# Softplus as one function, and a 512-to-2048 stage in two passes over its weights, in a fused attention and two-MLP kernel

## The chip, the cores and the metric

One core of a Trainium2 chip. The metric is the device time of one execution in microseconds; the time of before is 829.03 us, the median of three runs (827.82 to 829.51).

## What is computed

Attention with a local window and 32 global tokens on 4 batches of 544 tokens, then two MLPs on the 2,176 tokens. Cut to what matters here:

```python
h = np.maximum(np.maximum(x @ w1, x @ w2), x @ w3)     # 512 -> 768
x = h @ w_out                                          # 768 -> 512
h = x @ w_in                                           # 512 -> 2048
g = np.maximum(h, 0.0) + np.log1p(np.exp(-np.abs(h)))  # softplus
out = g @ w_out2                                       # 2048 -> 512
```

The kernel computes 2,176 tokens (the first 2,176 rows of the reference's batch-by-token order). Its weights reach it as 64-bit floats and are made into pairs of 32-bit words on the chip.

## The kernel before

Every matrix operand is kept as two fp32r parts, high and low: `split` makes the high part with a copy (ScalarE, in short ACT, or VectorE, in short DVE) and the low part with a subtraction on GpSimd (in short POOL). A product is three TensorE (PE) matmuls: high by high, high by low, low by high.

The order of all instructions is written by hand (`tc.manual_schedule()`); each engine runs its queue in that order, and all DMAs are issued from SyncE's queue (SP). Work on the side is a Python generator, from which the main loops take a step now and then: `wide(x)` adds x to a debt and takes a step for each whole one, and the constants `WU`, `WD`, `VL`, `VE` are such rates.

The stages, in time: attention (`att_stream`) beside the conversion of the first MLP's weights (`dec_stream`) and its first blocks; the first MLP by blocks u of 256 or 288 tokens, `up` (768 wide, three weights, 12 matmuls for each of 18 products, accumulated in a bank of pool `pm`; `rest` takes the maximum, L527) and `down`; beside them `words` converts the second MLP's weights, whose words go to DRAM (`qd`). When attention is over, blocks 6 and 7 run together, and on the side:

- `dec_w4` makes the 512-to-2048 weights. They come as eight pairs p; of each it reads a tile of four quarters, makes sums on DVE (L676, L677, L683, L691) and splits seven operands, as Strassen's scheme with seven products in place of eight wants them. All eight are done before the next stage, in 28 buffers of pools `cp` (8) and `wp` (24).
- `load_o(t)` makes the token operands of block t (544 tokens, four blocks): four DMAs, four sums on DVE, seven splits.

Then the 512-to-2048 stage, called the z stage here: 32 iterations i over (t, j) = divmod(i, 8), token block outside, weight pair inside. An iteration is 42 matmuls of 272 columns: `prods_a(i)` (three products into three PSUM banks za, zb, zc; copy e on ACT, first add L960), `prods_c(i - 1)` (two products; adds L968, L969), `prods_b(i)` (two products; adds L981, L982 in `mid_b`). The softplus of 4 x 272 columns is Abs (`abs_a` on za, `abs_h` on the three sums h), then Exp and Ln over 1,088 columns (L992, L993), then on DVE a max with zero and an add (`fin`, L999 and L1000), which also reads za from PSUM two iterations later. The result `a` is written to DRAM (`gd`). During block t, `load_o(t + 1)` runs beside it over eight iterations.

During the last eight iterations `make_v` makes the operands of the last matrix (2048 to 512), also eight pairs of seven operands: `vread` loads, `vsum` makes four sums (DVE for the first two pairs, POOL for the other six), `vsplit` splits; here `hi_on` puts the high parts on DVE until the z stage ends.

The last stage walks `items` (token block tb of 256 tokens, pair p), blocks 0 and 1 interleaved first, then 2 to 8. For each, `sums` makes token operands (L1098 to L1100 on DVE, copies L1105 on ACT, subtractions L1106 on DVE) about three items ahead of `mults`, 21 matmuls of 256 columns; after a block's eighth item `evac` adds up its seven products and writes the output. Two blocks take all eight PSUM banks, so the third waits for the first one's evacuation.

Of the kernel before, what the change touches and what calls it, by code (L numbers as in the profile page):

```python
# [21 lines left out]
def body(ctx, tc, kq, vw, vb, qg, w1, w2, w3, w_out, w2_in, w2_out, out):  # L22
# [483 lines left out]
    def up(u, f, i):  # L506
        n = 256 + 32 * (u % 2)
        xh, xl = xs[u]
        need((i, f))
        w = W[i, f].rearrange("p t (k f) -> p t k f", k=4)  # L510
        p = pm.tile([128, 512], F32, tag="m", name="pu")[:, 0:n]
        for k in range(4):
            nc.tensor.matmul(p, lhsT=w[:, 0, k], rhs=xh[:, k, 0:n], start=(k == 0), stop=False)  # L513
            nc.tensor.matmul(p, lhsT=w[:, 0, k], rhs=xl[:, k, 0:n], start=False, stop=False)  # L514
            nc.tensor.matmul(p, lhsT=w[:, 1, k], rhs=xh[:, k, 0:n], start=False, stop=(k == 3))  # L515
        pend.append((u, f, i, n, p))
        while len(pend) > lag[0]:
            rest()
# [77 lines left out]
    wd, w4_done = [False], [False]  # L596
# [62 lines left out]
    def dec_w4():  # L659
        half = None  # L660
        qs = {}

        def read(p):
            qs[p] = dp.tile([128, 4, 256], F32, tag="raw", name="qi", bufs=3)
            nc.sync.dma_start(out=qs[p].rearrange("p a n -> p (a n)"), in_=qd["i"][p].rearrange("p a n -> p (a n)"))

        read(0)
# [35 lines left out]
        w4_done[0] = True  # L703

    def load_o(t, pool, temp):
        x = ob[t] = pool.tile([128, 7, 2, 2, 272], F32R, tag="o", name="o7", bufs=1)
        b12, b11, b22 = [temp() for _ in range(3)]
# [3 lines left out]
        yield  # L711
        split(x[:, 0], b11)
        yield
        nc.vector.tensor_tensor(b11, b12, b11, op=ALU.subtract)
        nc.vector.tensor_tensor(b12, b22, b12, op=ALU.subtract)
        split(x[:, 2], b22)
        yield
        split(x[:, 3], b11)
        yield
        nc.vector.tensor_tensor(b11, b22, b11, op=ALU.subtract)  # L720
        nc.sync.dma_start(out=b22, in_=od[t][:, 2:4, 0:272])
        split(x[:, 5], b12)
        yield
        split(x[:, 4], b11)
        yield
        split(x[:, 1], b22)
        yield
        nc.vector.tensor_tensor(b22, b22, b11, op=ALU.subtract)
        split(x[:, 6], b22)
        yield  # L730

    def early_temp():
        return dp.tile([128, 2, 272], F32, tag="tmp", name="ot", bufs=3)

    def late_temp():
        return wp.tile([128, 2, 272], F32, tag="w", name="ot")

    with tc.manual_schedule():
# [3 lines left out]
        cp = sp = None  # L742
# [11 lines left out]
        VD = 2.2  # L754
# [3 lines left out]
        VL = 2.8  # L758
        PV = 2
        VE = 1.6  # L760
# [94 lines left out]
        for u in range(6):  # L855
# [10 lines left out]
            for c in range(4):  # L866
# [7 lines left out]
                wide(VD)  # L874
# [16 lines left out]
        d4, lo0 = dec_w4(), load_o(0, op0, early_temp)  # L891
# [21 lines left out]
        for f, _ in enumerate(down_all(7)):  # L913
            if f < 6:
                free4[0] += 1
            wide(WD)
        for _ in lo0:
            pass
        need4(7)
# [5 lines left out]
        de = dctx.enter_context(tc.tile_pool(name="de", bufs=3, side="left"))  # L925
        op1 = dctx.enter_context(tc.tile_pool(name="op1", bufs=1, side="left"))

# [16 lines left out]
        gw = []  # L944

# [4 lines left out]
        def prods_a(i):  # L950
            t, j = divmod(i, 8)
# [19 lines left out]
        def prods_b(i):  # L971
# [4 lines left out]
            c["a"] = da.tile([128, 4, 272], F32, tag="a", name="a", bufs=4)  # L976
# [7 lines left out]
        def abs_a(i):  # L984
            nc.scalar.activation(pr[i]["a"][:, 0], pr[i]["z"][0], AF.Abs)

        def abs_h(i):
            nc.scalar.activation(pr[i]["a"][:, 1:4], pr[i]["h"], AF.Abs)
# [6 lines left out]
        def fin(i):  # L995
            c = pr.pop(i)
            t, j = divmod(i, 8)
# [7 lines left out]
        items = [(0, 0), (0, 1), (0, 2), (1, 0), (0, 3), (1, 1), (0, 4), (1, 2), (0, 5), (1, 3), (0, 6), (1, 4), (0, 7), (1, 5), (1, 6), (1, 7)]  # L1005
        items += [(tb, p) for tb in range(2, 9) for p in range(8)]
# [12 lines left out]
        def vsum(p):  # L1019
            e = nc.vector if p < PV else nc.gpsimd  # L1020
            q = vq[p]
            s = vs[p] = wp.tile([128, 4, 256], F32, tag="w", name="vs")
            e.tensor_tensor(s[:, 0:2], q[:, 0:4:2], q[:, 1:4:2], op=ALU.add)
            e.tensor_tensor(s[:, 2], q[:, 0], q[:, 3], op=ALU.add)
            e.tensor_tensor(s[:, 3], q[:, 1], q[:, 3], op=ALU.subtract)
            e.tensor_tensor(q[:, 2], q[:, 2], q[:, 0], op=ALU.subtract)

        def vsplit(p):
            q, s = vq.pop(p), vs.pop(p)
            if p == 0:  # L1030
                vs["o"] = op0.tile([128, 2, 7, 2, 256], F32R, tag="o", name="v01", bufs=1)
            if p < 2:
                v = [vs["o"][:, p, i] for i in range(7)]
                both = [vs["o"][:, p, i:i + 2] for i in (0, 2, 4)]
# [5 lines left out]
            for x, y in zip(both, (q[:, 0:4:3], s[:, 0:2], s[:, 2:4])):  # L1040
                split(x.rearrange("p a t n -> p t a n"), y, hi_on[0])
                yield
            split(v[6], q[:, 2], hi_on[0])
# [3 lines left out]
        hi_on = [nc.vector]  # L1047

        def make_v():
            vread(0)  # L1050
            vread(1)
            yield
            vsum(0)
            yield
            vsum(1)
            yield
            while op0_free[0] == 0:
                yield
            for p in range(8):
                if 0 < p < 7:  # L1060
                    vread(p + 1)
                g = vsplit(p)
                next(g)
                yield
                next(g)
                yield
                if 0 < p < 7:
                    vsum(p + 1)
                    yield
                for _ in g:  # L1070
                    yield

        op0_free = [0]
# [118 lines left out]
        vdebt = [0.0]  # L1192
        for i in range(32):
            t, j = divmod(i, 8)
            if j == 0:
                for _ in nxt:
                    pass
                nxt = load_o(t + 1, (op1, op0)[t % 2], late_temp) if t < 3 else iter(())
            prods_a(i)
            if i > 1:  # L1200
                exps(i - 2)
            if i > 0:
                prods_c(i - 1)
            if i > 1:
                fin(i - 2)
            if j > 0:
                next(nxt, None)
            if i > 0:
                abs_h(i - 1)
            prods_b(i)  # L1210
            abs_a(i)
            mid_b(i)
            if j > 1:
                next(nxt, None)
            if t == 2 and j >= 5:
                next(vgen, None)
            if t == 3:
                op0_free[0] = 1
                vdebt[0] += VL
                while vdebt[0] >= 1 and j > 0:  # L1220
                    vdebt[0] -= 1
                    next(vgen, None)
                if j >= 3:
                    ahead(j - 2)
                    if j > 4:
                        prep(j - 5)
                        start(j - 4)
        exps(30)
        prods_c(31)
        fin(30)  # L1230
        abs_h(31)
        exps(31)
        fin(31)
# [6 lines left out]
        hi_on[0] = None  # L1240
        for i, x in enumerate(items):
# [8 lines left out]
            mults(*x)  # L1250
            next(ev, None)
            if x[0] < 2:
# [59 lines left out]
```

## Time and profile before

| | |
|---|---|
| median of three runs | 829.03 us |
| the profiled execution | 830.44 us |
| its span | 828.7 us |
| PE busy | 771.2 us (93%) |
| DVE busy | 644.2 us (78%) |
| ACT busy | 413.9 us (50%) |
| POOL busy | 239.6 us (29%) |

The span goes from the first to the last instruction of the program; 1.74 us of the profiled execution lie outside it. Busy time is the union of an engine's instructions. The rows below come from the page of the profile, from windows (busy time of each engine in a stretch, with the clock that TensorE was granted, 1.00 for 2.4 GHz), from lists of waits, from instructions grouped by line, and from single instructions in order of time.

### The profile page before, as it was taken

How to read it: one execution, taken by the hardware profiler on the slowest of the kernel's cores; microseconds unless marked ns; L12 is line 12 of the kernel's file. 1: busy time of each engine (PE TensorE's matmuls, PEld its weight loads, DVE VectorE, ACT ScalarE, POOL GpSimd, SP SyncE). 2: the span in 40 equal slices, each digit the busy share in tenths (PEclk: the TensorE clock that was granted, in tenths of full speed). 3: DMA queues.
4: the chain of work that ended last, by engine and by line, in shares of the span. 5: the costliest groups of instructions: out<-in, count | busy, mean ns of one | idle time of the engine just before them, and what ended most of it. 6: DMA issues, size and time to landing. Idle time of an engine off the chain costs nothing.

```text
span 828.7 us, 18140 instructions
## 1 busy us (share of the span) xinstructions
PE 771.2 (93%) x6984; PEld 735.3 (89%) x6984; DVE 644.2 (78%) x1536; ACT 413.9 (50%) x966; POOL 239.6 (29%) x222
## 2 busy tenths in 40 slices
PE   5799998999999999999999999999966798999998
PEld 3589997999989899999999999999966688999998
DVE  6968965888976876329963768677999989999995
ACT  6854446545534422034444777777644344444442
POOL 4534431222111100009950404031875730000000
PEclk9989999999999999999999999999979989999999
DMA  9857128777686645050302343433553413343432
GB/s 338 320 194 267 47 87 266 236 266 253 231 263 218 205 146 174 7 173 29 116 26 73 118 149 116 146 114 149 189 176 137 149 51 102 127 129 127 128 90 77
DMA packets 73959, 128.72 MB, mean 155 GB/s; under 512 B 9488, under 2 KB 43152, under 8 KB 73872
## 3 DMA queue, kind: packets, MB, share of 16 engines
q1 hardware_dynamic: 73872, 127.56, 45.1%
q8 instruction: 55, 0.90, 0.4%
q14 instruction: 32, 0.26, 0.1%
HBM read 89.06 MB, written 38.47 MB: 154 GB/s over the span
## 4 chain that ended last, share of the span: by engine, by line
PE 65%; DVE 20%; DMA 4%; issue 4%; ACT 4%; POOL 1%; SPq 1%; DVEq 0%; POOLq 0%; ACTq 0%
PE pu L513 6%; PE pu L515 6%; PE pu L514 6%; PE z L1112 6%; PE z L1110 6%; PE z L1111 6%; PE z L939 4%; PE z L941 4%; PE z L940 4%; PE pd L560 2%; PE pd L559 2%; PE pd L561 2%; DVE sm L1098 2%; DVE oo L1106 2%; PE ps L142 2%
## 5 line engine op out<-in xcount | busy, mean ns | idle before, releaser
L513 PE MATMUL pu<-xh,w 128*128 128x256 f32 (+1 forms) x576 | 171.5, 298 | 4.3 <-DVE m L527 2.2
L515 PE MATMUL pu<-xh,w 128*128 128x256 f32 (+1 forms) x576 | 168.2, 292 | 0.8 <-POOL w L451 0.8
L514 PE MATMUL pu<-xl,w 128*128 128x256 f32 (+1 forms) x576 | 168.6, 293 | 0.2
L1110 PE MATMUL z<-v,oo 128*128 128x256 f32 x480 | 138.8, 289 | 10.7 <-ACT oo L1105 8.0
L1112 PE MATMUL z<-v,oo 128*128 128x256 f32 x480 | 139.3, 290 | 5.3 <-DVE oo L1106 5.3
L939 PE MATMUL z<-o,wi 128*128 128x272 f32 x448 | 132.2, 295 | 11.6 <-ACT e L959 5.4
L1111 PE MATMUL z<-v,oo 128*128 128x256 f32 x480 | 138.5, 289 | 0.0
L941 PE MATMUL z<-o,wi 128*128 128x272 f32 x448 | 130.4, 291 | 0.0
L940 PE MATMUL z<-o,wi 128*128 128x272 f32 x448 | 130.3, 291 | 0.0
L513 PEld LDWEIGHTS pu<-xh,w 128*128 128x128 f32 x576 | 110.8, 192 | 8.5 <-DVE m L527 3.4
L515 PEld LDWEIGHTS pu<-xh,w 128*128 128x128 f32 x576 | 110.6, 192 | 1.2 <-POOL w L451 1.2
L514 PEld LDWEIGHTS pu<-xl,w 128*128 128x128 f32 x576 | 110.9, 193 | 0.6 <-DVE xl L114 0.6
L1110 PEld LDWEIGHTS z<-v,oo 128*128 128x128 f32 x480 | 94.3, 197 | 12.4 <-ACT oo L1105 9.5
L1105 ACT ACTIVATE oo<-sm 128x640 fp32r<-128x640 f32 (+1 forms) x72 | 49.7, 691 | 109.6 <-DVE sm L1100 103.7
L1112 PEld LDWEIGHTS z<-v,oo 128*128 128x128 f32 x480 | 94.1, 196 | 6.7 <-DVE oo L1106 6.7
L939 PEld LDWEIGHTS z<-o,wi 128*128 128x128 f32 x448 | 86.0, 192 | 15.5 <-ACT e L959 6.7
L1111 PEld LDWEIGHTS z<-v,oo 128*128 128x128 f32 x480 | 93.9, 196 | 0.0
L941 PEld LDWEIGHTS z<-o,wi 128*128 128x128 f32 x448 | 85.8, 191 | 0.0
L940 PEld LDWEIGHTS z<-o,wi 128*128 128x128 f32 x448 | 85.7, 191 | 0.0
L164 POOL TENSOR_TENSOR s<-s,rs 128x512 f32<-128x512 f32 x32 | 36.2, 1133 | 159.9 <-DVE rs L162 92.6
L648 POOL TENSOR_TENSOR o<-ot,o 128x544 fp32r<-128x544 f32 x28 | 43.0, 1537 | 96.4 <-PE z L941 65.4
L1106 DVE TENSOR_TENSOR oo<-sm,oo 128x640 fp32r<-128x640 f32 (+1 forms) x72 | 58.8, 816 | 14.4 <-ACT oo L1105 10.8
(152 smaller groups left out, 1750.2 us busy)
## 6 DMA issues: line engine op xcount, KB each, us to landing
gd<-a SPq DMA_DIRECT2D x32, 544.0 KB, 2.8
gl<-gd SPq DMA_DIRECT2D x32, 512.0 KB, 5.6
kq<-in_kq_dram SPq DMA_DIRECT2D x31, 448.0 KB, 5.7
raw<-in_w_out_dram SPq DMA_DIRECT2D x22, 512.0 KB, 4.6
raw<-in_w_dram SPq DMA_DIRECT2D x18, 512.0 KB, 7.5
vt<-in_vw_dram SPq DMA_DIRECT2D x16, 512.0 KB, 6.0
raw<-in_w_in_dram SPq DMA_DIRECT2D x16, 512.0 KB, 4.6
ot<-od SPq DMA_DIRECT2D x16, 272.0 KB, 3.7
```

Of the source, the lines that this page charges most:

```text
L513: nc.tensor.matmul(p, lhsT=w[:, 0, k], rhs=xh[:, k, 0:n], start=(k == 0), stop=False)
L514: nc.tensor.matmul(p, lhsT=w[:, 0, k], rhs=xl[:, k, 0:n], start=False, stop=False)
L515: nc.tensor.matmul(p, lhsT=w[:, 1, k], rhs=xh[:, k, 0:n], start=False, stop=(k == 3))
L648: nc.gpsimd.tensor_tensor(w[:, 1], src, w[:, 0].bitcast(F32), op=ALU.subtract)
L939: nc.tensor.matmul(z, lhsT=w[:, 0, k], rhs=x[:, 0, k], start=st and k == 0, stop=False, skip_group_check=True)
L940: nc.tensor.matmul(z, lhsT=w[:, 0, k], rhs=x[:, 1, k], start=False, stop=False, skip_group_check=True)
L941: nc.tensor.matmul(z, lhsT=w[:, 1, k], rhs=x[:, 0, k], start=False, stop=sp and k == 1, skip_group_check=True)
L1105: nc.scalar.activation(oh[:, a:b], src, AF.Copy)
L1106: nc.vector.tensor_tensor(ol[:, a:b], src, oh[:, a:b].bitcast(F32), op=ALU.subtract)
L1110: nc.tensor.matmul(p, lhsT=oh[:, a], rhs=w[:, 0], start=st, stop=False, skip_group_check=True)
L1111: nc.tensor.matmul(p, lhsT=oh[:, a], rhs=w[:, 1], start=False, stop=False, skip_group_check=True)
L1112: nc.tensor.matmul(p, lhsT=ol[:, a], rhs=w[:, 0], start=False, stop=sp, skip_group_check=True)
```

## The change

- Softplus is one ACT function, on za right after `prods_b` and on h one iteration later; Exp, Ln and `fin`'s two DVE instructions go, and its table set is loaded once, when attention is over. `a` has three buffers instead of four.
- `dec_w4` makes pairs 0 to 3 before the z stage and pairs 4 to 7 in the stage's first half.
- The z stage goes over `order`: pairs 0 to 3 for token blocks 0, 1, 2, 3, then pairs 4 to 7 for blocks 2, 3, 1, 0. `load_o` runs five times, over four iterations each.
- `make_v` starts with the second half: pairs 0 to 3 in the buffers of the dead weight pairs, 4 and 5 in a dead token operand, 6 and 7 when the z stage is over. High parts are on ACT, all `vsum` on DVE.
- The last stage takes the 256-token blocks as 7, 6, ... 0, 8, and its first item's matmuls are put ahead of the last iteration's `prods_c`.
- In blocks 6 and 7 of `up`, the third product of each three takes its PSUM bank from a new pool of two; the tile `s` of `dec_w4` has one buffer instead of two.

```diff
@@ up
-        p = pm.tile([128, 512], F32, tag="m", name="pu")[:, 0:n]
+        p = (pe if pe and i == 2 else pm).tile([128, 512], F32, tag="m", name="pu")[:, 0:n]
@@ split
-    def split(w, src, hi=None):
-        if hi is None:
-            nc.scalar.activation(w[:, 0], src, AF.Copy)
-        else:
-            hi.tensor_copy(w[:, 0], src)
+    def split(w, src):
+        nc.scalar.activation(w[:, 0], src, AF.Copy)
@@ dec_w4
-        for p in range(8):
-            if p < 7:
-                read(p + 1)
+        for p in ps:
             q = qs.pop(p)
-            s = sp.tile([128, 2, 256], F32, tag="s", name="s")
+            s = sp.tile([128, 2, 256], F32, tag="s", name="s", bufs=1)
...
             split(wc.rearrange("p a t n -> p t a n"), q[:, 1:3])
+            if p < ps[-1]:
+                read(p + 1)
@@ before the z stage
+        nc.scalar.preload_act_table_set("softplus")
+        pe = mo_ctx.enter_context(tc.tile_pool(name="pe", bufs=2, space=PSUM))
+        d4 = dec_w4(range(4), lambda: dp.tile([128, 4, 256], F32, tag="raw", name="qi", bufs=3))
...
+        free4[0] = 24
+        d5 = dec_w4(range(4, 8), lambda: wp.tile([128, 4, 256], F32, tag="w", name="qi"))
-        need4(7)
+        need4(3)
@@ softplus
-        def exps(i):
-            a = pr[i]["a"]
-            nc.scalar.activation(a, a, AF.Exp, scale=-1.0)
-            nc.scalar.activation(a, a, AF.Ln, bias=1.0)
+        def soft_a(i):
+            nc.scalar.activation(pr[i]["a"][:, 0], pr[i]["z"][0], AF.Softplus)
+
+        def soft_h(i):
             c = pr.pop(i)
-            t, j = divmod(i, 8)
+            t, j = order[i]
             a = c["a"]
-            nc.vector.scalar_tensor_tensor(a[:, 0], c["z"][0], 0.0, a[:, 0], op0=ALU.max, op1=ALU.add)
-            nc.vector.scalar_tensor_tensor(a[:, 1:4], c["h"], 0.0, a[:, 1:4], op0=ALU.max, op1=ALU.add)
+            nc.scalar.activation(a[:, 1:4], c["h"], AF.Softplus)
@@ order
+        order = [(t, j) for t in range(4) for j in range(4)] + [(t, j) for t in (2, 3, 1, 0) for j in range(4, 8)]
+        blocks = [7, 6, 5, 4, 3, 2, 1, 0, 8]
@@ vsum
-            e = nc.vector if p < PV else nc.gpsimd
+            e = nc.vector
@@ the loop of the z stage
+        fresh = {0: (1, op1), 4: (2, op0), 8: (3, op1), 20: (1, op0), 24: (0, op1)}
         for i in range(32):
+            k = i % 4
...
             prods_a(i)
             if i > 0:
                 prods_c(i - 1)
+                soft_h(i - 1)
+            next(nxt, None)
+            prods_b(i)
+            soft_a(i)
+            mid_b(i)
+            next(nxt, None)
+            if k:
                 next(nxt, None)
+            for _ in range(1 + (k == 1)):
+                next(d5, None)
+            if i >= 16:
+                if i == 28:
+                    vgate[0] = 1
+                vdebt[0] += VD if i < 28 else VL
+                while vdebt[0] >= 1:
                     vdebt[0] -= 1
                     next(vgen, None)
+            if i == 29:
+                ahead(2)
+            elif i > 29:
+                prep(i - 30)
+        vgate[0] = 2
+        mults(*items[0])
         prods_c(31)
+        soft_h(31)
+        prep(2)
```

`VD` is 2.6, `VL` 3.5 and `VE` (steps of `make_v` for each item of the last stage) 1.4, after 1.6. A pair of `make_v` has seven steps, three sums and four splits.

## Rows read from the trace of the kernel before

**Rows 1.** The page, part 1: span, and PE's busy us, share and instructions.
```profile
span 828.7 us, 18140 instructions
PE 771.2 (93%) x6984; PEld 735.3 (89%) x6984; DVE 644.2 (78%) x1536; ACT 413.9 (50%) x966; POOL 239.6 (29%) x222
```
**Rows 2.** Windows: length, busy of PE, PEld, DVE, ACT, POOL, clock, DMA, GB/s.
```profile
439.86:580.00 140.14, 137.73 (x1077) 135.27 (x1078) 98.63 (x194) 100.45 (x145) 32.35 (x21) 1.00 0.35 127
580.00:626.74 46.74, 38.04 (x269) 36.84 (x268) 46.18 (x77) 26.67 (x40) 34.70 (x29) 0.89 0.55 183
626.74:700.00 73.26, 57.27 (x395) 54.16 (x394) 66.11 (x109) 31.07 (x59) 33.92 (x28) 0.88 0.33 105
700.00:825.60 125.60, 125.60 (x1049) 125.40 (x1047) 111.37 (x293) 54.52 (x114) 0.00 (x0) 1.00 0.36 114
```
**Rows 3.** Timeline of PE (start, us): first z matmul, first and last of the last stage.
```profile
439.86 0.39 PE L939 MATMUL z<-o,wi 128*128 128x272 f32 x1 [0.50 <-ACT o L584]
...
626.74 0.28 PE L1110 MATMUL z<-v,oo 128*128 128x256 f32 x1
...
825.32 0.28 PE L1112 MATMUL z<-v,oo 128*128 128x256 f32 x1
```
**Rows 4.** Timeline of DVE: the first add of iterations 1, 3 and 25.
```profile
445.46 0.44 DVE L960 TENSOR_TENSOR h<-e,z 128x272 f32<-128x272 f32 x1 [0.65 <-PE z L941]
...
455.95 0.44 DVE L960 TENSOR_TENSOR h<-e,z 128x272 f32<-128x272 f32 x1 [0.55 <-PE z L941]
...
576.90 0.44 DVE L960 TENSOR_TENSOR h<-e,z 128x272 f32<-128x272 f32 x1 [0.44 <-PE z L941]
```
**Rows 5.** PE's waits, 580 to 700 us: total us, times, longest.
```profile
PE z L1110 <- ACT oo L1105: 8.0, 7, 3.5
PE z L939 <- ACT e L959: 5.4, 1, 5.4
PE z L1112 <- DVE oo L1106: 5.3, 7, 2.1
PE z L1110 <- DVE o L1155: 2.7, 1, 2.7
```
**Rows 6.** Groups by line, 440 to 580 us: count, busy us, mean ns, idle before.
```profile
L1000 DVE SCALAR_TENSOR_TENSOR a<-h,a 128x816 f32<-128x816 f32 x24 | 26.1, 1086 | 0.0
L999 DVE SCALAR_TENSOR_TENSOR a<-z,a 128x272 f32<-128x272 f32 x24 | 10.5, 436 | 4.6 <-ACT a L993 4.6
L1023 DVE TENSOR_TENSOR vs<-vq 128x512 f32<-128x512 f32 x2 | 1.4, 686 | 0.0
L1026 DVE TENSOR_TENSOR vq<-vq 128x256 f32<-128x256 f32 x2 | 0.8, 422 | 0.0
...
L993 ACT ACTIVATE a<-a 128x1088 f32<-128x1088 f32 x24 | 26.8, 1115 | 0.8
L992 ACT ACTIVATE a<-a 128x1088 f32<-128x1088 f32 x24 | 26.6, 1106 | 0.0
```
**Rows 7.** Groups by line: the one table load on ACT.
```profile
L739 ACT ACT_TABLE_LOAD x1 | 1.3, 1283 | 0.8 <-PEq L1301 0.8
```
**Rows 8.** PE's waits, 380 to 480 us, the longest.
```profile
PE pu L513 <- DVE m L527: 2.2, 4, 0.9
```
**Rows 9.** Groups by line, 580 to 700 us: a split's low half on POOL.
```profile
L648 POOL TENSOR_TENSOR v<-vs,v 128x512 fp32r<-128x512 f32 x16 | 24.5, 1532 | 16.7 <-ACT v L645 12.0 <-DVE v L647 4.7
```
**Rows 10.** Groups by line beside POOL work, 380 to 480, then 580 to 700 us.
```profile
L676 DVE TENSOR_TENSOR s<-qi 128x256 f32<-128x256 f32 x6 | 8.1, 1358 | 0.0
...
L1098 DVE TENSOR_TENSOR sm<-gl 128x256 f32<-128x256 f32 x22 | 20.6, 935 | 0.0
```
**Rows 11.** Timeline of DVE: the first and last of ten such subtractions, one an item.
```profile
643.28 0.82 DVE L1106 TENSOR_TENSOR oo<-sm,oo 128x640 fp32r<-128x640 f32 x1 [0.47 <-ACT oo L1105]
...
680.39 0.83 DVE L1106 TENSOR_TENSOR oo<-sm,oo 128x640 fp32r<-128x640 f32 x1 [0.47 <-ACT oo L1105]
```
**Rows 12.** Windows, columns as in rows 2: the stretch between those two.
```profile
643.28:680.39 37.11, 29.42 (x192) 26.93 (x191) 33.83 (x46) 14.48 (x30) 22.91 (x19) 0.88 0.33 102
```

More of the change, by code (lines that the diff above doesn't have):

```diff
@@ L700, in dec_w4 @@
             split(wc.rearrange("p a t n -> p t a n"), q[:, 1:3])
+            if p < ps[-1]:
+                read(p + 1)
             yield
             wi[p] = [wa[:, 0], wa[:, 1], h, wb[:, 0], wb[:, 1], wc[:, 1], wc[:, 0]]
-        w4_done[0] = True
     def load_o(t, pool, temp):
         x = ob[t] = pool.tile([128, 7, 2, 2, 272], F32R, tag="o", name="o7", bufs=1)
-        b12, b11, b22 = [temp() for _ in range(3)]
+        b12, b11, b22 = [temp(i) for i in range(3)]
+        t1 = sp.tile([128, 2, 272], F32, tag="t", name="t1", bufs=1)
         for r, k, c in ((b11, 0, 0), (b12, 0, 1), (b22, 2, 1)):
@@ L711, in load_o, with early_temp @@
         yield
+        nc.vector.tensor_tensor(t1, b12, b11, op=ALU.subtract)
         split(x[:, 0], b11)
         yield
-        nc.vector.tensor_tensor(b11, b12, b11, op=ALU.subtract)
         nc.vector.tensor_tensor(b12, b22, b12, op=ALU.subtract)
+        split(x[:, 3], t1)
+        yield
         split(x[:, 2], b22)
         yield
[L718 to L721, printed above, removed]
+        nc.vector.tensor_tensor(b11, b22, t1, op=ALU.subtract)
         split(x[:, 5], b12)
         yield
+        nc.sync.dma_start(out=b22, in_=od[t][:, 2:4, 0:272])
         split(x[:, 4], b11)
         yield
+        yield
         split(x[:, 1], b22)
+        nc.vector.tensor_tensor(b12, b22, b11, op=ALU.subtract)
         yield
-        nc.vector.tensor_tensor(b22, b22, b11, op=ALU.subtract)
-        split(x[:, 6], b22)
+        split(x[:, 6], b12)
         yield
-    def early_temp():
+    def early_temp(i):
         return dp.tile([128, 2, 272], F32, tag="tmp", name="ot", bufs=3)
-    def late_temp():
-        return wp.tile([128, 2, 272], F32, tag="w", name="ot")
     with tc.manual_schedule():
@@ L757, in body @@
         GW = 1
-        VL = 2.8
-        PV = 2
-        VE = 1.6
+        VD = 2.6
+        VL = 3.5
+        VE = 1.4
         LG = 3
@@ L912, in body @@
             wide(WD)
-        for f, _ in enumerate(down_all(7)):
-            if f < 6:
-                free4[0] += 1
+        for _ in down_all(7):
             wide(WD)
@@ L925, in body, with late_temp @@
         de = dctx.enter_context(tc.tile_pool(name="de", bufs=3, side="left"))
+        dt = dctx.enter_context(tc.tile_pool(name="dt", bufs=2, side="left"))
         op1 = dctx.enter_context(tc.tile_pool(name="op1", bufs=1, side="left"))
+        def late_temp(i):
+            if i == 0:
+                return wp.tile([128, 2, 272], F32, tag="w", name="ot")
+            return dt.tile([128, 2, 272], F32, tag="t", name="ot")
         def zt(shape):
@@ L975, in prods_b @@
             product(zb, w[5], x[5], False, False)
-            c["a"] = da.tile([128, 4, 272], F32, tag="a", name="a", bufs=4)
+            c["a"] = da.tile([128, 4, 272], F32, tag="a", name="a", bufs=3)
         def mid_b(i):
@@ L1003, in fin @@
                 write_g()
-        items = [(0, 0), (0, 1), (0, 2), (1, 0), (0, 3), (1, 1), (0, 4), (1, 2), (0, 5), (1, 3), (0, 6), (1, 4), (0, 7), (1, 5), (1, 6), (1, 7)]
-        items += [(tb, p) for tb in range(2, 9) for p in range(8)]
+        blocks = [7, 6, 5, 4, 3, 2, 1, 0, 8]
+        items = [(0, 0), (0, 1), (0, 2), (0, 3), (1, 0), (0, 4), (1, 1), (0, 5), (1, 2), (0, 6), (1, 3), (0, 7), (1, 4), (1, 5), (1, 6), (1, 7)]
+        items = [(blocks[a], p) for a, p in items] + [(tb, p) for tb in blocks[2:] for p in range(8)]
         gl, ops, mb, xe, xo = {}, {}, {}, None, None
@@ L1023, in vsum @@
             e.tensor_tensor(s[:, 0:2], q[:, 0:4:2], q[:, 1:4:2], op=ALU.add)
+            yield
             e.tensor_tensor(s[:, 2], q[:, 0], q[:, 3], op=ALU.add)
             e.tensor_tensor(s[:, 3], q[:, 1], q[:, 3], op=ALU.subtract)
+            yield
             e.tensor_tensor(q[:, 2], q[:, 2], q[:, 0], op=ALU.subtract)
+            yield
         def vsplit(p):
             q, s = vq.pop(p), vs.pop(p)
[L1030 to L1034, printed above, removed]
+            if p == 4:
+                vs["o"] = op0.tile([128, 2, 7, 2, 256], F32R, tag="o", name="v45", bufs=1)
+            if p in (4, 5):
+                v = [vs["o"][:, p - 4, i] for i in range(7)]
+                both = [vs["o"][:, p - 4, i:i + 2] for i in (0, 2, 4)]
             else:
@@ L1040, in vsplit @@
             for x, y in zip(both, (q[:, 0:4:3], s[:, 0:2], s[:, 2:4])):
-                split(x.rearrange("p a t n -> p t a n"), y, hi_on[0])
+                split(x.rearrange("p a t n -> p t a n"), y)
                 yield
-            split(v[6], q[:, 2], hi_on[0])
+            split(v[6], q[:, 2])
             V[p] = v
             yield
-        hi_on = [nc.vector]
         def make_v():
             vread(0)
-            vread(1)
             yield
[L1053 to L1058, printed above, removed]
-            for p in range(8):
-                if 0 < p < 7:
-                    vread(p + 1)
[L1062 to L1068, printed above, removed]
+            for p in range(8):
+                while vgate[0] < (p > 3) + (p > 5):
+                    yield
+                for _ in vsum(p):
+                    yield
+                if p < 7:
+                    vread(p + 1)
+                for _ in vsplit(p):
                     yield
-                for _ in g:
-                    yield
-        op0_free = [0]
+        vgate = [0]
         vgen = make_v()
@@ L1249, in body @@
                 next(vgen, None)
-            mults(*x)
+            if i > 0:
+                mults(*x)
             next(ev, None)
-            if x[0] < 2:
+            if i < 16:
                 next(ev, None)
```

57 lines of the change are left out of this document (11 added, 46 removed).

## The prediction

> **What bounds the kernel now.** I read the page first: TensorE (PE) is busy 771.2 of 828.7 us and no other engine comes near it [rows 1], so a change can only win where PE is not running or runs at the lower clock. The windows by stage show where that is [rows 2]. Up to 580 us PE is busy 137.7 of 140.1 us at a granted clock of 1.00; after 700 us it is busy 125.6 of 125.6. Between them, 580 to 700, it is busy 95.3 of 120 us, the granted clock falls to 0.89 and 0.88, and VectorE (DVE) is busy 112.3 of 120: DVE is the bound there.
>
> How much is lost is counted against PE's own pace. The 512-to-2048 stage (the z stage) has 32 iterations of 42 matmuls, from 439.86 to 626.74 us [rows 3]. Undisturbed, two iterations take 10.49 us (the h add of L960 at 445.46 and two iterations on at 455.95 [rows 4]), 5.25 each, so 32 need 168.0 us; they took 186.9, a loss of 18.9. Of it 5.5 us come by 576.90, the add of iteration 25 (131.4 us after iteration 1, for 24 x 5.25 = 126.0 [rows 4]); the other 13 lie in the last six iterations. The last stage has 1,440 matmuls at 125.6/1,049 = 0.1197 us [rows 2], 172.4 us; from 626.74 to 825.60 they took 198.9 [rows 3], a loss of 26.5. PE's waits of 580 to 700 say who is late: the token operands oo, from ScalarE (ACT) and DVE, 8.0 and 5.3 us; one ACT copy held up 5.4; the evacuation add L1155 2.7 [rows 5]. Idle time and the slow restarts at the lower clock are both in these losses. With none left the span would be 828.7 - 18.9 - 26.5 = 783.3.
>
> **Part by part.**
>
> Softplus. Abs, Exp, Ln on ACT and max-plus-add on DVE (L999, L1000) become one function. Per iteration DVE loses 0.44 + 1.09 = 1.53 us and ACT 1.11 + 1.12 = 2.23 us [rows 6]. By itself this frees 49 us of DVE in the stage and moves PE only where DVE is late. It also ends za's PSUM bank one iteration sooner: its last reader is now the first Softplus, not L999. Softplus has no row. I price it as the two Abs whose place it takes: Exp and Ln, unlike functions, cost alike on the same 1,088 elements, 1.12 and 1.11 us [rows 6]. That is the low end; the high end is all three functions that it stands for, some 3.4 us an iteration. ACT has room for either, being busy 100.5 of 140 us with the three [rows 2]: I count 0.
>
> The new table set costs a load on ACT; the one load of before took 1.28 us [rows 7]. It falls at the start of the last pair of 512-to-768 blocks, where ACT is not what PE waits for [rows 8]: 0, and 1.3 us if that cover is gone. The Trainium skill (ScalarE: Activation LUTs, What ACT_TABLE_LOAD costs) counts a drain as well, about 2.7 us a switch; by it an uncovered load would add 2.7. The row shows the load's own time alone.
>
> Before the z stage. Only four of the eight weight pairs are made there, and the third of each three up-products gets two banks of its own. Against this the s tile has one buffer instead of two, so DVE's next L676 can wait for POOL's split of the last one, and the max of L527 is queued behind it. PE's waits there for that max are 2.2 us in four places [rows 8]. I take -1.5, from -3.5 (all, with the restarts) to +2 (each of three pairs waits half a POOL instruction of 1.5 us [rows 9]).
>
> The z stage in two passes. PE's matmuls are the same ones in another order: 168.0 us. Moved into it are the sums and splits of four weight pairs, two more loads of token operands (five, not three, now with four iterations' time each instead of eight), and the making of six of the eight pairs of the last matrix; its high halves go from DVE to ACT, its sums from POOL to DVE. DVE's load: five adds of 0.44 an iteration, 70 us; 16 ops of 256 elements, 20 of 544, and six pairs' vsum of 0.69 + 3 x 0.42 = 1.95 us [rows 6]. In quiet that is 6.7 + 14.6 (544 taken by the 512-element row) + 11.7 = 33, in all 103 of 168 us. But these have both inputs in SBUF and run beside POOL's splits, where the same form took 1.36 and 0.94 us instead of 0.42 [rows 10]; by these they cost 22 + 32 + 26 = 80, in all 150 of 168. POOL has 35 + 35 splits at 1.53 at most [rows 9], 107 us. So none of the engines is the bound on average, and PE loses only where work clusters: iterations 1, 5 and 9, with three load steps and two weight steps, and those at which a vsum meets a load. The nearest rows are the first 24 iterations of before, where DVE was 70% busy and 5.5 us went in 131 [rows 2, 4]: at that rate 7 in 168. DVE's load lies between 61 and 89%, with more slack per add; I take 6, from 1 to 15 (five loads at 3 us). What is queued behind a late DVE op: L960's add, which PE's second za/zb products wait for. On SyncE's queue two more loads of four DMAs and four reads stand between the writes of g; a slot not free there holds those writes, and with three buffers for a instead of four the Softplus behind them. I count it in the 15.
>
> The turn into the last stage. The first item's products are put ahead of the last iteration's c-products, 2.5 us of PE work over the wait for the last adds. Reversing the blocks costs nothing: blocks 7 and 6, read first, are complete after the first half of the second pass, block 0 has all other blocks for cover.
>
> The last stage. Two pairs are left to make: 2 x 3.5 splits x 1.53 = 10.7 us of POOL work [rows 9] beside the DVE ops that make PE's operands. An item needs 21 x 0.1197 = 2.51 us of PE. Beside POOL, nine items took DVE 37.11 us, from 643.28 to 680.39 [rows 11], for 22.6 of PE: 14.5 lost, at 22.91 us of POOL work [rows 12], 0.63 for each. So 6.8 us, up to 10.2 if the pair before trails into it; the two vsums add 3.9 on DVE, and three items made ready ahead give back two items, 5.0. That is 5.7 to 9.1. A DVE that lags also evacuates late, and the second pair of blocks then waits once, as 2.7 before [rows 5]. I take 8.5, from 3 (no wait, POOL half hidden) to 14.
>
> The sum: 783.3 - 1.5 + 6 + 8.5 = 796.3 us of span, and the 1.74 us around it (830.44 - 828.7) give 798.0 against the profiled run's 830.44. That run lies 1.41 over the median of those shown, 829.03, so the forecast is **797 us**. Its own range, the bounds combined without taking all at one end, is 788 to 806.
>
> **The rivals.**
>
> *Nothing clusters.* The freed 49 us of DVE absorb the moved work, and the lead holds: z loses 2, the last stage 3, the earlier part gains 3. 783.3 + 2 + 3 - 3 + 0.3 = 786. For it: DVE's quiet sum of 61%. Against: 5.5 us went at 70%.
>
> *DVE and POOL block each other throughout.* The 60 DVE ops of the z stage each meet a split of POOL and wait for it whole, about 1 us more (1.36 against 0.42 [rows 6, 10]), and the makers of operands fall behind: DVE's 163 of 168 us leave no slack, PE follows DVE, z loses 20 and the last stage 14: 797 + 14 + 5 = 816 at worst, 810 in the middle. For it: POOL is twice as busy in the stage as before. Against: POOL rests about a third of it. The Trainium skill (SBUF — State Buffer, Who interferes with whom) states that a DVE instruction with two SBUF inputs and a GpSimd instruction that reads SBUF exclude each other, the later one waiting the other out; by that rule this rival would hold, and the trace agrees with 0.42 against 1.36 us.
>
> *The last matrix is not made in the second pass after all*: a buffer or gate holds it, and its splits fall into the last stage as before, with its 26.5 us lost: 797 + 18 = 815. Against: the pairs 0 to 3 are dead by then, 14 buffers.
>
> *Slower: Softplus is a slow function.* Up to 580 us ACT's 100.5 us less 53.4 for Exp and Ln [rows 2, 6], over 26.7 iterations, are 1.8 an iteration, 0.7 without the two Abs at Exp's price; 49 more splits at half of Exp's 1.11 (544 elements) add 0.9. So 3.6 of the 5.25 us are left for Softplus. Beyond that ACT sets the pace, and at 4.6 us, four times Exp's price, the 33 us of gain are used up; at 5.5 the time is 797 + 32 x 1.9 = 858. Against it: Exp and Ln cost alike.
>
> **How the numbers follow.** Forecast 0.60; nothing clusters 0.13; mutual blocking 0.17; not moved 0.06; slow Softplus 0.04. The likeliest gives 797. From 786 to 812 lie nearly all of the first, half of the second and most of the third: 0.8. A measurement here tells 0.2%, 1.7 us, from no change; all but the last case are faster by more: 0.95, within 0.01, slower 0.04.
>
> **What would show it.** Right: no run of PE waits between 580 and 625, the granted clock near 1.00 through the z stage, Softplus rows at about the pace of Exp, last-stage losses within its first 16 items and only beside POOL splits. Wrong: waits on z by Softplus (slow function), DVE over 90% busy in the z stage with L1023-like ops near 1.5 us (blocking), POOL splits of v long into the last stage (not moved), or a PE stall at the turn of over 5 us, which the lead of three items should exclude.

## The result, and the profile after

The changed kernel takes 808.47 us (median of four runs, 807.21 to 809.22) against 828.96 us for the kernel before, measured beside it (four runs): a ratio of 0.9753 [0.9736, 0.977], 20.5 us faster. The forecast of 797 us was 11.5 us too low. The result lies above the forecast's own range of 788 to 806; the range of 786 to 812, which takes in most of the rival of mutual blocking, holds it.

The page of the changed kernel, part 1 (columns as in rows 1):

```profile
span 807.0 us, 18054 instructions
PE 761.6 (94%) x6984; PEld 728.7 (90%) x6984; DVE 601.6 (75%) x1486; ACT 362.3 (45%) x935; POOL 231.4 (29%) x212
```

DVE shed 42.6 us and ACT 51.6, but PE still spends 45 us of the span not running. Windows of the changed kernel show where: the z stage (from its first matmul to the first of the last stage), the last stage up to 660 us, and the rest (columns as in rows 2):

```profile
433.74:617.70 183.96, 173.03 (x1332) 171.58 (x1333) 126.04 (x221) 83.00 (x167) 94.14 (x71) 0.97 0.48 165
617.70:660.00 42.30, 35.33 (x259) 32.49 (x258) 38.56 (x73) 20.19 (x40) 19.68 (x12) 0.97 0.47 151
660.00:803.95 143.95, 143.83 (x1197) 143.62 (x1196) 130.75 (x344) 64.43 (x134) 0.00 (x0) 1.00 0.35 111
```

The last 144 us run without a gap, as in the last line of rows 2. The rest of the loss lies beside POOL's work. Because the turn mixes matmuls of both stages, I count losses from here on matmul by matmul: what the distance to the next start exceeds 0.1253 us in the z stage and 0.1197 in the last. (Most neighbours in the z stage lie 0.125 us apart, so its losses are counted 0.4 us too low, in every kernel alike; differences between kernels are not touched.) Before, that gives 18.5 and 26.3 us (the prediction had 18.9 and 26.5 from the stages' ends); after, 17.1 and 12.1. So the last stage gave 14.2 us and the z stage only 1.4. The stretch from matmul 3,600 to the first z matmul went from 82.90 to 80.56 us, 2.3 less. The other 3.8 us are in the first 87 us of the program, where no instruction was changed; the last section shows that they come of the clock.

PE's waits in the z stage, and then from 617 to 700 us (total us, times, longest):

```profile
PE z L943 <- DVE h L965: 10.1, 5, 2.8
...
PE z L1099 <- DVE oo L1093: 4.0, 8, 2.0
PE z L1098 <- POOL v L645: 1.3, 2, 1.1
PE z L1097 <- ACT oo L1092: 0.9, 2, 0.7
PE z L1097 <- ACT v L644: 0.7, 1, 0.7
```

ACT's 8.0 and 5.4 us of waits [rows 5] have all but gone. In their place stand five waits for one DVE instruction, the first add of an iteration (L960 before, L965 now), at 448.85, 472.99, 497.10, 567.55 and 587.89 us. The first three follow the load's and weights' steps of iterations 1, 5 and 9; the other two come where a `vsum` meets a load. Here is DVE around the second, then POOL over the same time (start, us):

```profile
464.56 0.72 DVE L709 TENSOR_TENSOR t<-ot 128x544 f32<-128x544 f32 x1
...
466.55 1.65 DVE L712 TENSOR_TENSOR ot<-ot 128x544 f32<-128x544 f32 x1
468.12 1.58 DVE L671 TENSOR_TENSOR s<-qi 128x256 f32<-128x256 f32 x1
469.73 1.45 DVE L672 TENSOR_TENSOR s<-s,qi 128x256 f32<-128x256 f32 x1
471.11 1.48 DVE L678 TENSOR_TENSOR qi<-qi 128x256 f32<-128x256 f32 x1
472.51 0.42 DVE L965 TENSOR_TENSOR h<-e,z 128x272 f32<-128x272 f32 x1
```
```profile
466.25 1.37 POOL L645 TENSOR_TENSOR o<-ot,o 128x544 fp32r<-128x544 f32 x1 [3.81 <-ACT o L644]
467.57 1.84 POOL L645 TENSOR_TENSOR o<-t,o 128x544 fp32r<-128x544 f32 x1
469.38 1.52 POOL L645 TENSOR_TENSOR o<-ot,o 128x544 fp32r<-128x544 f32 x1
470.87 2.31 POOL L645 TENSOR_TENSOR wi<-qi,wi 128x512 fp32r<-128x512 f32 x2
```

L709 and L712 are the same operation on the same shape. With POOL idle it takes 0.72 us, beside POOL's subtraction 1.65. From there on each DVE sum is about as long as a split, and the first three end 0.3 to 0.6 us behind the end of one (467.62, 469.41, 470.90). L965, which has one of its two inputs in PSUM, takes its usual 0.42 us beside a split: it is late only because four sums queue ahead of it. Over 436 to 660 us this holds without exception: of the 134 DVE operations with two inputs in SBUF, 61 lie beside a POOL split, and 45 of these take over 0.15 us more than in quiet; of the other 73 none does. Of the adds with an input in PSUM 77 lie beside a split, and none takes over 0.44 us. PE then loses more than the 2.79 us of the wait. Its timeline:

```profile
472.99 0.39 PE L943 MATMUL z<-o,wi 128*128 128x272 f32 x1 [2.79 <-DVE h L965]
473.22 0.38 PE L944 MATMUL z<-o,wi 128*128 128x272 f32 x1
...
476.56 0.34 PE L944 MATMUL z<-o,wi 128*128 128x272 f32 x1
476.75 0.29 PE L945 MATMUL z<-o,wi 128*128 128x272 f32 x1
476.87 0.29 PE L943 MATMUL z<-o,wi 128*128 128x272 f32 x1
```

For 3.76 us after the wait 17 matmuls start 0.22 us apart, at a granted clock of 0.55 (nearly all of it at the 1.2 GHz level); at 0.1253 they would take 2.13. That is 1.6 us on top. The waits of 1.88 and 2.73 us have such a stretch behind them too, those of 1.36 and 1.37 have none; together they explain most of what the z stage lost beyond its waits.

### The profile page after: what moved, and what is told of

The parts are those of the page before. It is cut to its first block, busy times and chain, and to the rows that moved or that the text cites. A ratio compares the mean times of both kernels' runs of the same rounds, so it can differ in the third digit from the quotient of the medians.

```text
span 807.0 us, 18054 instructions
## 1 busy us (share of the span) xinstructions
PE 761.6 (94%) x6984; PEld 728.7 (90%) x6984; DVE 601.6 (75%) x1486; ACT 362.3 (45%) x935; POOL 231.4 (29%) x212
## 4 chain that ended last, share of the span: by engine, by line
PE 76%; DVE 12%; issue 3%; ACT 3%; DMA 3%; POOL 2%; SPq 0%; POOLq 0%; ACTq 0%; DVEq 0%
PE pu L513 8%; PE pu L514 8%; PE pu L515 8%; PE z L1098 6%; PE z L1099 6%; PE z L1097 6%; PE z L943 6%; PE z L945 6%; PE z L944 6%; PE pd L560 2%; PE pd L561 2%; PE pd L559 2%; DMA raw<-in_w_dram 2%; PE pog L294 2%; PE ps L142 2%
## 5 line engine op out<-in xcount | busy, mean ns | idle before, releaser
L513 PE MATMUL pu<-xh,w 128*128 128x256 f32 (+1 forms) x576 | 169.4, 294 | 1.5 <-ACT xo L255 1.0
L515 PE MATMUL pu<-xh,w 128*128 128x256 f32 (+1 forms) x576 | 166.9, 290 | 0.8 <-POOL w L451 0.8
L943 PE MATMUL z<-o,wi 128*128 128x272 f32 x448 | 131.7, 294 | 11.4 <-DVE h L965 10.1
L1099 PE MATMUL z<-v,oo 128*128 128x256 f32 x480 | 137.1, 286 | 4.0 <-DVE oo L1093 4.0
L1098 PE MATMUL z<-v,oo 128*128 128x256 f32 x480 | 136.7, 285 | 1.3 <-POOL v L645 1.3
L1097 PE MATMUL z<-v,oo 128*128 128x256 f32 x480 | 135.9, 283 | 1.7 <-ACT oo L1092 0.9
L513 PEld LDWEIGHTS pu<-xh,w 128*128 128x128 f32 x576 | 109.3, 190 | 4.8 <-ACT xo L255 1.2
L515 PEld LDWEIGHTS pu<-xh,w 128*128 128x128 f32 x576 | 109.0, 189 | 1.2 <-POOL w L451 1.2
L514 PEld LDWEIGHTS pu<-xl,w 128*128 128x128 f32 x576 | 109.2, 190 | 0.8 <-DVE xl L114 0.6
L1099 PEld LDWEIGHTS z<-v,oo 128*128 128x128 f32 x480 | 91.6, 191 | 5.6 <-DVE oo L1093 5.6
L1097 PEld LDWEIGHTS z<-v,oo 128*128 128x128 f32 x480 | 92.1, 192 | 2.5 <-ACT oo L1092 1.6
L1098 PEld LDWEIGHTS z<-v,oo 128*128 128x128 f32 x480 | 91.5, 191 | 1.7 <-POOL v L645 1.7
L645 POOL TENSOR_TENSOR o<-ot,o 128x544 fp32r<-128x544 f32 x36 | 51.2, 1434 | 68.4 <-DVE h L986 38.9
L996 ACT ACTIVATE a<-h 128x816 f32<-128x816 f32 x32 | 28.4, 887 | 92.7 <-DVE h L974 92.7
```

Source lines behind the costliest of these rows:

```text
L943: nc.tensor.matmul(z, lhsT=w[:, 0, k], rhs=x[:, 0, k], start=st and k == 0, stop=False, skip_group_check=True)
L1097: nc.tensor.matmul(p, lhsT=oh[:, a], rhs=w[:, 0], start=st, stop=False, skip_group_check=True)
L1098: nc.tensor.matmul(p, lhsT=oh[:, a], rhs=w[:, 1], start=False, stop=False, skip_group_check=True)
L1099: nc.tensor.matmul(p, lhsT=ol[:, a], rhs=w[:, 0], start=False, stop=sp, skip_group_check=True)
```

## The experiments

The theory was that each collision of a two-input DVE sum with a POOL split holds DVE for the split's whole length, and that PE loses where several such sums stand ahead of the z stage's first add. The rivals put the missing time into the order of the second pass, POOL's own lateness, the turn, or a mispriced Softplus.

**One part alone: Softplus in the old order** (before, with this alone):

```diff
-            nc.scalar.activation(pr[i]["a"][:, 0], pr[i]["z"][0], AF.Abs)
+            nc.scalar.activation(pr[i]["a"][:, 0], pr[i]["z"][0], AF.Softplus)
...
-            nc.vector.scalar_tensor_tensor(a[:, 0], c["z"][0], 0.0, a[:, 0], op0=ALU.max, op1=ALU.add)
-            nc.vector.scalar_tensor_tensor(a[:, 1:4], c["h"], 0.0, a[:, 1:4], op0=ALU.max, op1=ALU.add)
+            nc.scalar.activation(a[:, 1:4], c["h"], AF.Softplus)
```

> The kernel before with one part of the change alone: Softplus as one ACT function in the place of Abs, with Exp, Ln and the two DVE instructions gone. Theory (DVE is late in the last six iterations of the z stage): each of them gets 1.5 us of DVE back, z loses 6 to 9 us instead of 18.9, the last stage keeps most of its 26.5, and the time is 813 to 820 us. Rival (the gain is that of the two passes; DVE's max and add were waiting time filled): 827 to 830 us.

Measured: 817.48 us against 828.82 (0.987 [0.9837, 0.9903]); losses 9.8 us in the z stage, a little over the 6 to 9 expected, and 23.4 in the last. So over half of the whole gain, 11.3 us, comes from DVE and ACT having less to do where they were late.

**The other part alone: two passes with the old softplus** (after, with Abs, Exp, Ln, the max and the add put back, and g's writes issued one step sooner since `a` is finished one iteration later):

```diff
-        GW = 1
+        GW = 0
...
-            nc.scalar.activation(pr[i]["a"][:, 0], pr[i]["z"][0], AF.Softplus)
+            nc.scalar.activation(pr[i]["a"][:, 0], pr[i]["z"][0], AF.Abs)
```

> The changed kernel with the old softplus (Abs, Exp, Ln, max and add), the result tile written out one step earlier so that three buffers do. Theory (DVE's slack in the z stage decides): 1.5 us more of DVE in each of 32 iterations lengthens every stall at which loads, weight sums and vsum meet, the z stage loses 25 to 40 us instead of 16, and the time is 818 to 832 us. Rival (the two passes alone carry the gain): 807 to 812 us.

Measured: 827.89 us (0.9987 [0.9969, 1.0004]); losses 28.9 us in the z stage, 15.8 in the last, and 1.8 where one follows the other. PE's waits, 440 to 640 us:

```profile
PE z L942 <- DVE h L964: 11.6, 7, 3.1
PE z L942 <- DVE h L985: 6.3, 6, 1.5
PE z L942 <- ACT e L963: 3.5, 3, 2.0
```

The two passes bring the last stage 10.5 us, and cost the z stage 10.4 and the turn 1.8; the stretch before the z stage is 4.0 us shorter (78.90 against 82.90). In the median they are worth nothing by themselves; Softplus makes the room that they need.

**POOL writes instead of reading.** The low halves, a POOL subtraction of two operands in SBUF, become a memset; in the second kernel three of them, so that POOL is busy as long as before:

```diff
-        nc.gpsimd.tensor_tensor(w[:, 1], src, w[:, 0].bitcast(F32), op=ALU.subtract)
+        nc.gpsimd.memset(w[:, 1].bitcast(F32), 0.0)
+        nc.gpsimd.memset(w[:, 1].bitcast(F32), 0.0)
+        nc.gpsimd.memset(w[:, 1].bitcast(F32), 0.0)
```

> The changed kernel with POOL's low-half subtractions of split replaced by POOL writing zeros into the same tiles: the low parts of the second MLP's weights and of the z stage's token operands are left out of the result. POOL then reads no SBUF, and DVE's work is the same. Theory (DVE operations with two inputs in SBUF are held up by POOL's reads): the 544-element DVE operations beside POOL go from 1.6 to 0.72 us and the 256-element ones from 1.5 to 0.42, z loses 2 to 5 us, the last stage 4 to 8, the time is 786 to 795 us. Rival (the number of DVE operations in a cluster, or POOL's own finishing time, is what stalls): the operations are as long as before or the time is 802 to 810 us.

> The changed kernel with each of POOL's low-half subtractions replaced by three writes of zeros into the same tile, some 1.6 us for 512 elements, so that POOL works as long as with the subtractions but reads no SBUF (the low parts are left out of the result, as with one write). Theory (POOL's reads hold up DVE): DVE's operations stay at 0.42 and 0.72 us and the time is 784 to 790 us, as with one write. Rival (what helped in the run with one write was POOL's shorter time): the time goes back to 800 us or more.

Measured: 785.23 us with one memset (0.9477 [0.944, 0.9515]) and 786.3 with three (0.9483 [0.9467, 0.95]); losses 1.0 us in the z stage in both, 3.8 and 3.9 in the last. Windows from 436 to 600 us, first of after, then of the kernel with three memsets:

```profile
436.00:600.00 164.00, 153.87 (x1185) 152.77 (x1184) 114.20 (x193) 75.08 (x151) 89.63 (x67) 0.97 0.45 156
```
```profile
436.00:600.00 164.00, 164.00 (x1312) 163.79 (x1310) 95.49 (x217) 82.10 (x165) 110.86 (x225) 1.00 0.53 183
```

POOL is busy 21 us longer and PE runs through. DVE does more work in 19 us less. By form over the same window (count, busy us, mean ns), after and then three memsets, whose lines lie two further down:

```profile
L712 DVE TENSOR_TENSOR ot<-ot 128x544 f32<-128x544 f32 x5 | 8.1, 1620 | 0.0
L671 DVE TENSOR_TENSOR s<-qi 128x256 f32<-128x256 f32 x4 | 5.7, 1413 | 0.0
```
```profile
L714 DVE TENSOR_TENSOR ot<-ot 128x544 f32<-128x544 f32 x5 | 3.6, 719 | 0.0
L673 DVE TENSOR_TENSOR s<-qi 128x256 f32<-128x256 f32 x4 | 1.7, 420 | 0.6 <-DMA qi<-qi 0.6
```

Over 436 to 660 us, 74 DVE operations with two inputs in SBUF lie beside a memset, and none is long. So it is not POOL's time and not the order of the passes that costs: it is POOL's reading while DVE reads two operands. A memset also leaves DVE no operand to wait for, but that is not what helps: the waits of the changed kernel's DVE from 433 to 660 us name PE and ACT and never POOL, and L712 shares no operand with the split beside it. With the reading gone the time is that of the rival *Nothing clusters*, 786 us.

**Other places for the weight sums.** Three, none, one and one step in four iterations instead of one, two, one, one, and no `vsum` step where a load's splits run:

```diff
-            for _ in range(1 + (k == 1)):
+            for _ in range((3, 0, 1, 1)[k]):
...
-                while vdebt[0] >= 1:
+                while vdebt[0] >= 1 and not (k == 1 and 20 <= i < 28):
```

> The changed kernel, with the same side work at other moments: the four steps of weight making that fell on iterations 0 and 1 of each four (1 and 2 of them) become 3 and 0, and make_v takes no step in the iterations 21 and 25, where the first splits of a load run. Theory (the five stalls of the z stage are clusters of DVE operations that each wait for a POOL split): those five stalls go, z loses 4 to 7 us instead of 16, the time is 797 to 802 us. Rival (DVE and POOL have too much work over the whole stage, and it meets PE elsewhere): 805 to 810 us.

Measured: 805.96 us (0.9742 [0.9707, 0.9778]); the z stage's loss falls from 17.1 to 11.4, the last stage's stays at 12.0. The time lies in the rival's range and its interval overlaps that of the changed kernel; the z stage's loss lies between the two expectations. In place of the five waits there are 0.44, 0.47, 0.50, 2.14 and 0.95 us, not all at the old places, but the earlier steps met a weight tile that had not landed, and PE waited 2.69 us at a new place, until 445.44, for ACT's copy e (L964). That copy stood behind a split's, which waited for the tile. ACT's timeline there:

```profile
444.48 0.63 ACT L644 ACTIVATE wi<-qi 128x512 fp32r<-128x512 f32 x1 [5.77 <-DMA qi<-qi]
445.01 0.38 ACT L964 ACTIVATE e<-z 128x272 f32<-128x272 f32 x1
```

**The last stage: low halves of pairs 6 and 7 on DVE.**

```diff
+        lo_on[0] = nc.vector   # when the z stage is over
...
-        nc.gpsimd.tensor_tensor(w[:, 1], src, w[:, 0].bitcast(F32), op=ALU.subtract)
+        lo_on[0].tensor_tensor(w[:, 1], src, w[:, 0].bitcast(F32), op=ALU.subtract)
```

> The changed kernel with the low halves of the two late pairs (6 and 7) subtracted on DVE instead of POOL; nothing else differs. Theory (in the last stage DVE loses more by waiting for POOL's splits than the splits would cost it): eight operations of 0.42 to 0.7 us are added to DVE, 5 us, the sums and subtractions of the first 16 items fall back to 0.42 and 0.82 us, the last stage loses 5 to 8 us instead of 12.1, the time is 801 to 805 us. Rival (DVE's own work is the bound there): 808 to 813 us.

Measured: 804.08 us (0.9696 [0.9681, 0.9712]); the last stage's loss falls from 12.1 to 6.5, the z stage's stays at 17.1. By form, 617 to 660 us, after and then this kernel:

```profile
L1093 DVE TENSOR_TENSOR oo<-sm,oo 128x640 fp32r<-128x640 f32 x12 | 12.0, 1002 | 3.0 <-ACT oo L1092 3.0
L1085 DVE TENSOR_TENSOR sm<-gl 128x256 f32<-128x256 f32 x13 | 9.8, 751 | 0.0
```
```profile
L1095 DVE TENSOR_TENSOR oo<-sm,oo 128x640 fp32r<-128x640 f32 x15 | 13.3, 889 | 1.6 <-ACT oo L1094 1.6
L1087 DVE TENSOR_TENSOR sm<-gl 128x256 f32<-128x256 f32 x14 | 5.8, 415 | 0.0
...
L647 DVE TENSOR_TENSOR v<-vs,v 128x512 fp32r<-128x512 f32 x4 | 2.7, 680 | 0.0
```

DVE took over eight splits, at 0.42 to 0.68 us each, and finished more items by 660 us than before. Its busy time over the span fell all the same, from 601.6 to 599.4 us: a split on POOL cost DVE more than the split itself.

**Both, with the sums ahead of the splits.** The low halves on DVE as above, the weight and `make_v` steps placed as in the respaced kernel, and besides: a load's two sums go ahead of its first split, pair 4's read is issued before the stage, and `make_v` takes four steps an iteration before iteration 20, then 1.7:

```diff
+        nc.vector.tensor_tensor(b12, b22, b12, op=ALU.subtract)
         split(x[:, 0], b11)
         yield
-        nc.vector.tensor_tensor(b12, b22, b12, op=ALU.subtract)
...
+        next(d5)
...
-                vdebt[0] += VD if i < 28 else VL
+                vdebt[0] += 4 if i < 20 else 1.7 if i < 28 else VL
```

> The run before this one and a new spacing of the z stage together: the first two DVE sums of a load stand ahead of its first split, pair 4's read is issued ahead of the stage, weight steps are 3, 0, 1, 1 in each four iterations, make_v runs at 4 steps an iteration before iteration 20, 1.7 to 27, none in 21 and 25. Theory (only DVE operations that meet a POOL split cost PE anything): z loses 5 to 9 us instead of 17, the last stage 5 to 8, the time is 789 to 796 us. Rival (the collisions only move): 800 to 806 us.

Measured: **790.36 us** (0.9531 [0.9505, 0.9557]); losses 3.6 and 6.4 us. It computes everything and beats both kernels. Its window over the same 164 us, and its waits from 440 to 700:

```profile
436.00:600.00 164.00, 162.48 (x1294) 161.68 (x1292) 110.24 (x216) 81.88 (x164) 91.89 (x72) 1.00 0.53 182
```
```profile
PE z L946 <- ACT e L967: 2.3, 2, 1.9
PE z L1102 <- DVE oo L1096: 1.5, 5, 0.4
```

DVE is still busy 110 us, 15 more than with memsets: many collisions remain. From 436 to 600 us 26 of 64 operations with two inputs in SBUF are long, by 18 us together; in the changed kernel it is 34 of 52, by 31 us. They no longer stand three or four in a row ahead of an add but at most two, and the z stage loses 3.6 instead of 17.1. How much of this each of the four new placements does was not tested; the respaced steps alone left 11.4.

**The turn without its cover.** The first item's products behind the last iteration's `prods_c`:

```diff
-        mults(*items[0])
         prods_c(31)
         soft_h(31)
         prep(2)
+        mults(*items[0])
```

> The changed kernel with the first item's products of the last stage behind the last iteration's c-products again. By the prediction these 2.5 us of PE work cover the wait for DVE's last adds: without it PE waits at the c-products and again for the second item, and the time is 1.5 to 3 us longer, 810 to 811. Rival (DVE's lateness sets the pace of the first items, so the order of PE's work there is of no account): 807.5 to 809.5 us.

Measured: 809.03 us (0.9761 [0.9744, 0.9777]) against 0.9753 for the whole change: no difference. PE's waits, 610 to 700 us, have one more of 0.5 us at the turn and 0.8 less on the operands:

```profile
PE z L1099 <- DVE oo L1093: 3.2, 8, 1.2
...
PE z L943 <- DVE h L986: 0.5, 1, 0.5
```

**Without the two extra PSUM banks** before the z stage:

```diff
-        p = (pe if pe and i == 2 else pm).tile([128, 512], F32, tag="m", name="pu")[:, 0:n]
+        p = pm.tile([128, 512], F32, tag="m", name="pu")[:, 0:n]
```

> The changed kernel without the pool of two PSUM banks for the third of each three up-products: all take pool pm's five again. From PE's 3,600th matmul to the first of the z stage before took 82.9 us and the changed kernel 80.6. Theory (the two banks let PE run on while DVE's max is late): the stretch goes back to 82 to 84 us, with waits of L513 on the max of L527 as before, and the time is 809 to 811 us. Rival (the gain there is that half of the weight making has left the stage): 80 to 81.5 us, and the time stays at 807 to 809.

Measured: 810.3 us against 829.47 (0.9775 [0.9749, 0.9802]); the stretch before the z stage takes 80.85 us (after 80.56, before 82.90). The wait of rows 8 is back in part:

```profile
PE pu L513 <- DVE m L527: 1.3, 2, 0.9
```

The banks take away that wait. The 80.56 us of the changed kernel understate what they give: its profile has a stretch at the 1.2 GHz level there (a granted clock of 0.83 from 360 to 370 us), which none of the other ten profiles has between 340 and 440 us. Three kernels with the banks and the same work in this stretch (respaced, low halves on DVE, the turn uncovered) took 79.25 to 79.54 us. So, from single profiles, the banks are worth some 1.4 us and the four weight pairs that left some 2.0. In the time it does not show: the intervals overlap.

## Why the prediction was right and where it was wrong

*What bounds the kernel.* Right: every microsecond of the 15.6 won from 440 us on came out of PE's losses beside late ACT and DVE work, and the clean stretches kept their pace.

*Softplus at 0 on ACT.* Right in price. ACT by form, 433 to 617 us (count, busy us, mean ns):

```profile
L996 ACT ACTIVATE a<-h 128x816 f32<-128x816 f32 x30 | 26.6, 887 | 87.9 <-DVE h L974 87.9
...
L990 ACT ACTIVATE a<-z 128x272 f32<-128x272 f32 x31 | 11.7, 378 | 1.7 <-PE z L945 1.7
```

That is 1.27 us an iteration, the low end of the bounds; the slow function would have needed 4.6 to use up the gain. The new table load took 1.28 us, and no wait of PE between 350 and 434 us is over 0.5: the cover held.

*Before the z stage: -1.5.* Right in sign; it was -2.3 in this profile, with a slow stretch of TensorE's clock in it, and about -3.5 in the three others with the same work there: some 2.0 from the smaller side work, 1.4 from the banks.

*The z stage: 6.* This is the term that failed: 17.1, above even its high bound of 15. The parts of the step were right. DVE's load lay between the bounds (70% of 436 to 600 us), the clusters stood at iterations 1, 5 and 9 and where a `vsum` meets a load, and the collision's price was in rows 6 and 10, 0.42 against 1.36 us. What failed was the last line of the step: "at that rate 7 in 168". The rate of 5.5 us in 131 came from a stretch as busy on DVE, but with POOL busy 32 of 140 us [rows 2] and no wait of PE over 0.52 us. Now POOL is busy 94 of 184, and four collisions in a row make one add 2.8 us late. The high bound, five loads at 3 us, was the better count: five waits, 10.1 us, and some 1.6 us of low clock behind each of the three longest. A busy share cannot tell an evenly loaded DVE from one with four blocked sums ahead of an add.

*Mutual blocking as a rival, 810 to 816.* Its mechanism is the one that acted, at part of its strength, and the losses of 17.1 and 12.1 us lie nearer to its 20 and 14 than to the forecast's 6 and 8.5. DVE's sums were longer by 31 us in the 164, not by the 60 that one microsecond for each of 60 sums makes, because not every sum met a split and some met the end of one. The rule that it leaned on is borne out: the Trainium skill (SBUF — State Buffer, Who interferes with whom) says that a DVE instruction with two SBUF inputs excludes a GpSimd instruction that reads SBUF, but not one that only writes; L712 took 1.62 us beside subtractions and 0.72 beside memsets. The rival's sign to look for, DVE over 90% busy, was a bad one: DVE was at 69% of the stage, and the time came to within 2 us of its 810. Two of the forecast's signs of being right failed: PE waited 2.73 us until 587.89, and the granted clock of the z stage was 0.97.

*The turn.* The 2.5 us of PE work do cover a wait for the last adds, of 0.5 us, and it is worth nothing in the time, because the operands oo of a following item come late whatever PE does. DVE of the changed kernel at the turn:

```profile
619.40 1.39 DVE L1087 TENSOR_TENSOR sm<-gl 128x128 f32<-128x128 f32 x1
620.89 1.34 DVE L1093 TENSOR_TENSOR oo<-gl,oo 128x256 fp32r<-128x256 f32 x1
622.16 1.88 DVE L1093 TENSOR_TENSOR oo<-sm,oo 128x640 fp32r<-128x640 f32 x1
```

These three took 0.28, 0.42 and 0.82 us a little later, with POOL idle. Here POOL splits pair 5, from 619.29 to 624.63; they are 3.1 us longer, and PE waits 1.97 us for them at 624.10.

*The last stage: 8.5.* Mis-sized at 12.1, within the bounds of 3 to 14. The place was right: no loss after 660 us, when POOL is done. The splits of pairs 6 and 7 turn an L1085 from 0.42 to 1.5 us, and the trailing pair 5 had taken its toll at the turn already, which the prediction had only in its high count (10.2 us, "if the pair before trails into it").

*The sum.* The two terms were short by 14.7 us together; 3.8 us at the start and 0.8 before the z stage went the other way, which leaves 10.1. With 0.6 by which the losses of before come out smaller matmul by matmul (44.8 us, not 45.4) that is the 10.7 us of the span above its 796.3. That it was not more is luck in part: no term foresaw the 3.8 us at the start, and they are not the change's.

## What to carry to other kernels

List the DVE instructions that read two operands from SBUF and fall beside a GpSimd instruction that reads SBUF, price each at the whole GpSimd instruction, and add them up between two deadlines rather than over a stage. Here moving such sums ahead of the splits, spreading the steps of weight making, reading one tile earlier, and putting the last splits onto DVE itself turned 808 us into 790 with the same work. A part that frees an engine and a part that loads it have to be judged together: Softplus alone gave 11 us, the second pass alone nothing, both 20.5.

## What the runs showed of the hardware beyond that

The first 87 us are the same work in both kernels, but PE's 800th matmul starts at 86.97 us in the profile before and at 82.90 in the one after. Windows of before and then of after, columns as in rows 2:

```profile
40.00:60.00 20.00, 17.51 (x192) 15.50 (x192) 12.69 (x42) 11.48 (x40) 7.27 (x9) 0.83 0.44 158
```
```profile
40.00:60.00 20.00, 17.04 (x213) 15.03 (x214) 15.63 (x49) 13.13 (x44) 9.12 (x10) 1.00 0.49 177
```

PE is short of work there, and the granted clock was 0.83 in one and 1.00 in the other; from 60 to 80 us it was 0.91 and 1.00. In the profile before TensorE ran three stretches at the 1.2 GHz level in the first 87 us, in that of after none. The nine experiments, which leave that part of the program alone too, fall into the same order. Matmul 800 (counted from 0) starts at 82.79 and 82.90 us in the two profiles without such a stretch, at 83.91 to 84.68 in the six with one, at 85.81 and 85.87 in the two with two, and at 86.97 in the one with three. So these 3.8 us are the clock's and not the change's: each such stretch goes with one to two microseconds. What decides how many of them a run has is not shown.
